# Lightning attention and a leaky-ReLU MLP on one core: the last two pairs taken together by banks and halves, and the fourth chunk's scores ahead of its key-value products

## The chip, the cores and the metric

The kernel runs on one core of a Trainium2 chip. Its time is the device time of one execution in microseconds (us). A run is one execution; a profiled execution gives the trace, whose times count from the start of its span. TensorE is PE (its weight loads PEld), VectorE DVE, ScalarE ACT, GpSimd POOL, and SP is the engine that issues most DMAs.

## The reference, cut

Two blocks follow one another. The attention has B, H, S, D = 4, 8, 768, 64 and works in blocks of 64 tokens with a decaying state:

```python
intra = einsum('bhic,bhjc->bhij', qb, kb) * Dmask          # scores, decayed
intra = einsum('bhij,bhjd->bhid', intra, vb)
inter = einsum('bhid,bhde->bhie', qb * lam_pow, kv_state)
out[:, :, sl] = intra + inter
kv_state = lam_block * kv_state + einsum('bhsd,bhse->bhde', kb * rev_pow, vb)
```

Its output, as x of 3072 tokens x 512, goes through the MLP:

```python
h = x @ w_in                      # 512 -> 2048
return maximum(0.01 * h, h) @ w_out   # 2048 -> 512
```

## The kernel before, in words

**Chunks, groups, pairs.** The attention goes by 24 chunks of 128 tokens, each with all 8 heads. Four chunks make a group of T = 512 tokens, six groups in all, and two groups make one of three rounds `pr`. The 2048 hidden units are 8 pairs `p` of 256 units.

**Number format.** Products of the MLP run in fp32r. An operand is split into a head, a low part and a middle part (`xh`, `xl`, `xm` for activations, `wh`, `wl`, `wm` for weights), and each product of the MLP is three matmuls, one per part.

**A chunk.** `load_kq` and `load_v` fetch its q, k, v on SP's queue. `transposes` turns k and q on PE and ACT copies them out (`kT`, `qT`, L429, L430); POOL scales k by its decay in place (L434). `scores(c)` then does two things in one PSUM tile `psc`: `go`, the 32 products of transposed k and q in its lower half, and `kv`, the 32 products of scaled k and v in its upper half. Which of the two is put first hangs on GOFIRST: chunks below it have `go` first. DVE takes the scores with the decay (`sc`, L467) and adds the state (L474), POOL scales the state (L477). `outputs(c)` multiplies `sc` by v and q by the state into `po`, from which ACT and DVE make the chunk's `xh`, `xl`, `xm` (L522, L523, L525). Chunks 0 to 3 are done one at a time (`alone`), later ones interleaved with the MLP's first product.

**The MLP.** `up(g, p)` is the first product (L716) with its leaky ReLU, whose result is stored to DRAM. It needs the pair's weights, which come as raw 64-bit words (`w_in`, L582) and are made into numbers by ACT (L603, L605, L607) and DVE (L609, L610, L618, L621, L636). The second product comes in two ways. `strassen` works on combinations of blocks, `plain(pr, p, gi)` on a pair as it is: `unit` loads the pair's activations for one half `gi` of the round (L815), ACT and DVE split them (L818, L821, L825) into a slot of a ring, and PE multiplies them by the pair's weights (L841): four banks c = 0 to 3, one for each 128 columns of the output, in each bank 2 x 3 matmuls of 512 columns, so 24 matmuls to a pair. The banks of `gi` = 1 are `b10`, `b2`, `b11`, `pt`.

**The end of a round.** With the last pair (p = 7) the banks are finished one by one. After each, `turn_out` has DVE transpose it from PSUM to SBUF (L909), and `store_out` writes the finished banks out by DMA (L920), four stores for each half m of 256 columns. For the very last round and half the banks go in the order 2, 3, 0, 1; banks 2 and 3 are stored together, then banks 0 and 1, and bank 1, which comes last, is done in two halves of 256 columns. These 16 stores are spread over SP, ACT and POOL by the table ENDS; all other stores go on ACT's queue.

**What sets the order of work.** Each step is put into a planner (`Plan.add`) with its engine, an estimated duration, the keys that it reads and writes, and a rank. `emit` goes through them by estimated time, each engine taking the step that can start first (rank and order of entry decide ties), and writes out the instructions in that order of estimated starts. A key names a whole tile or bank: a step waits, by the estimate, for the last writer of a key that it reads and for the readers of one that it writes. Where PE would stand still by the estimate, filler transposes (L275) are put in. The waits on the chip are set by the tiles and places that the instructions touch, in the order in which they were written out.

Of the kernel before, what the change touches and what calls it, by code (L numbers as in the profile page):

```python
# [25 lines left out]
S = 4096.0  # L26
# [10 lines left out]
class Plan:  # L37
# [23 lines left out]
    def add(self, eng, us, fn, reads=(), writes=(), rank=0.0):  # L61

        n, deps = len(self.ops), set()
        for k in reads:
            w, r = self.last.setdefault(k, [None, []])
            if w is not None:
                deps.add(w)
            r.append(n)
        for k in writes:
            w, r = self.last.setdefault(k, [None, []])  # L70
            if w is not None:
                deps.add(w)
            deps.update(r)
            self.last[k] = [n, []]
        deps.discard(n)
        ways = {eng: us} if isinstance(eng, str) else dict(zip(eng, us))
        if self.slack:
            self.more[n] = self.slack
        if self.chain is not None:
            self.chains[self.chain].append(n)  # L80
        self.ops.append((ways, fn, deps, (self.rank + rank, n), set(writes)))
# [81 lines left out]
def kernel(  # L163
# [10 lines left out]
    nc = tc.nc  # L174
    P = 128
# [6 lines left out]
    NP = d_ff // (2 * P)  # L182
    NCH = B * NCB
    GC = 4
    NG = NCH // GC
    T = GC * C
# [6 lines left out]
    TURN = 3  # L193
    SLACK, GSLACK = 4.0, 2.0
    EARLY_SLACK = 1.0
    GOFIRST = 3
    SUBL, FIRST = 0.75, -8.0

    NS = 4
    LEAD = 8.0  # L200
# [4 lines left out]
    C4 = P // 4  # L205
# [32 lines left out]
    HT = T // 2  # L238
# [42 lines left out]
    add = plan.add  # L281
# [160 lines left out]
    def scores(c):  # L442
# [16 lines left out]

        if c < GOFIRST:  # L460
            add("PE", 0.47, go, [f"kT{i}", f"qT{i}"], ["psc"])
# [322 lines left out]
    acc = {"X": flat[:2], "Z": flat[2:], "Y": [b1[0], b2], "V": [b1[1], bank["pt"]]}  # L784
    ACC = {"X": ["X0", "X1"], "Z": ["Z0", "Z1"], "Y": ["b10", "b2"], "V": ["b11", "pt"]}
# [9 lines left out]
    BANKS = [[("X", 0), ("X", 1), ("Z", 0), ("Z", 1)], [("Y", 0), ("Y", 1), ("V", 0), ("V", 1)]]  # L795
# [72 lines left out]
    def plain(pr, p, gi, lead, last=False, banks=None):  # L868

        g = 2 * pr + gi  # L870
        here = plan.rank
        plan.rank -= lead
        d = G[pr][p].rearrange("p (f h t) -> p f h t", f=2, h=2)[:, :, gi, :]
        j = unit(d, [x for x in plan.last if x[0] == "G" and x[1] in (str(2 * pr), str(2 * pr + 1)) and x[2:4] == f"{p}{gi}"], 2)
        plan.rank = here
        reads = [f"r{z}{j}" for z in "hlm"] + [f"w{z}{p}" for z in "hlm"]

        def go(fs, cs, lo=0, n=T):
            for f in fs:
                for c in cs:  # L880
                    d, i = BANKS[gi][c]
                    product(acc[d][i][:, lo:lo + n], j, f * T + lo,
                            lambda z, f=f, c=c: W[p][z][:, f * 2 * NQ + c * P:f * 2 * NQ + (c + 1) * P], first=pr == p == f == 0, n=n)

        if not last:
            add("PE", 0.227 * 24, lambda: go((0, 1), range(4)), reads, [ACC[d][i] for d, i in BANKS[gi]])
            return
        end = pr == NG // 2 - 1 and gi == 1
        for i, c in enumerate(banks):
            d, b = BANKS[gi][c]  # L890
            parts_ = 2 if end and i == 3 else 1
            for half in range(parts_):
                k = ACC[d][b] + (f"half{half}" if parts_ > 1 else "")
                n = T // parts_
                add("PE", 0.227 * 6 * (1.0 if parts_ == 1 else 0.53), lambda c=c, half=half, n=n: go((0, 1), (c,), half * n, n),
                    reads + ([ACC[d][b]] if parts_ > 1 else []), [k])
                turn_out(c, acc[d][b], [ACC[d][b], k], half * n, n)
                if i == 3 or end and i == 1:
                    cs = sorted(banks[:2] if end and i == 1 else banks[2:] if end else banks)
                    for m in ([half] if parts_ > 1 else range(2)):  # L900
                        store_out(pr, gi, m, cs, end)

    otile = gst.rearrange("p x f (b c j) -> p (x f b) c j", c=4, j=C4)

    def turn_out(c, b, keys, lo, n):
        nonlocal n_o
        n_o += 1
        o = otile[:, lo // C4:(lo + n) // C4, c, :]
        add("DVE", 0.1 + 0.6 * n / T, lambda: nc.vector.transpose(out=o, in_=b[:, lo:lo + n].rearrange("p (b i) -> p b i", i=C4)), keys,  # L909
            [f"o{c}{m}" for m in range(lo // HT, (lo + n) // HT)] + (["gs0", "gs1"] if n_o <= 4 else []), rank=-1.5)  # L910

    def store_out(pr, gi, m, cs, last):
        t0, n, w = (2 * pr + m) * T + gi * HT, HT // C4, len(cs) * C4

        ENDS = {(8, 0): "PSAP", (8, 1): "PSAP", (4, 0): "SAPP", (4, 1): "SASA"}
        QUEUES = {"S": ("DMA", 0.5, nc.sync), "A": ("ACT", 0.5, nc.scalar), "P": ("POOL", 0.65, nc.gpsimd)}

        def store(a, q):
            c0 = a * P + cs[0] * C4
            q.dma_start(out=out[t0:t0 + HT, c0:c0 + w].rearrange("(b i) j -> i b j", i=C4),  # L920
                        in_=otile[a * C4:(a + 1) * C4, m * n:(m + 1) * n, cs[0]:cs[-1] + 1, :].rearrange("i b c j -> i b (c j)"))

        for a in range(4):
            e, us, q = QUEUES[ENDS[8 if cs[0] > 1 else 4, m][a] if last else "A"]
            add(e, us, lambda a=a, q=q: store(a, q), [f"o{c}{m}" for c in cs], [], rank=-1.5 if last else 6.0)

    def copy_banks(d, s):
        for i in range(2):
# [2 lines left out]
    def add_banks(d, s):  # L931
        for i in range(2):
            y, key = w32[:, i, :], [f"w32{i}"]
            add("ACT", 0.6, lambda i=i, y=y: nc.scalar.copy(y, acc[s][i]), [ACC[s][i]], key, rank=-LEAD)
            add("DVE", 0.72, lambda i=i, y=y: nc.vector.tensor_tensor(acc[d][i], acc[d][i], y, op=ALU.add), key, [ACC[d][i]], rank=-LEAD)

    seq = [("a", 0), ("a", 1), ("a", 2), ("a", 3), ("wi", 1), ("b", 4), ("r", 4), ("up", 0, 1), ("wi", 0), ("r", 5),
# [26 lines left out]
    for pr in range(NG // 2):  # L964
# [3 lines left out]
        def n(p, gi, r=pr):  # L968
            return ("n", r, p, gi) if p < NP - 1 else ("l", r, p, gi, (0, 1, 2, 3) if gi == 0 else (2, 3, 0, 1))
# [6 lines left out]
        else:  # L976
            i = seq.index(("up", NG - 1, NP - 1))
            seq[i:i] = [n(0, 0)]
            seq += [n(0, 1), n(1, 0), n(1, 1), ("ws", 0), n(2, 0), n(2, 1), ("ws", 1), n(3, 0), n(3, 1), ("ws", 2), n(4, 0), n(5, 0), ("ws", 3), n(6, 0), n(7, 0)]
    seq += [n(p, 1) for p in range(NS, NP)]  # L980

    freed = False
    for n, x in enumerate(seq):
        plan.rank = float(n)
        steady = begin <= n and x[0] in ("r", "up", "wo")
        if x[0] in "abr":
            {"a": alone, "b": begun, "r": round_of}[x[0]](x[1])
        elif x[0] == "ls":
            load_subs(DV)
            turn(DV)  # L990
        elif x[0] == "lt":
            load_subs(sum(run(DV)))
        elif x[0] == "wi":
            w_in(x[1])
        elif x[0] == "up":
            up(*x[1:])
        elif x[0] == "wo":
            w_out(*x[1:])
        elif x[0] == "wp":
            if not freed:  # L1000
                add("DVE", 0.0, lambda: None, [], ["psc", "po", "X0", "X1", "Z0", "Z1"])
                freed = True
            w_out_parts(x[1])
        elif x[0] == "ws":
            if x[1] == 0:
                add("DVE", 0.0, free_attention, [], ATT + [f"e{z}{p}" for z in "hlm" for p in range(NS)])
            w_sums(x[1])
        elif x[0] == "fr":
            add("ACT", 0.0, free_raws, [], [f"raw{i}" for i in range(NRAW)] + ["rh4", "rl4", "rm4", "zr"])
        elif x[0] == "s":  # L1010
            strassen(*x[1:], LEAD)
        elif x[0] == "n":
            plain(*x[1:], LEAD)
        elif x[0] == "copy":
            copy_banks(*x[1:])
        elif x[0] == "add":
            add_banks(*x[1:])
        else:
            plain(*x[1:4], LEAD, True, x[4])
    plan.emit()  # L1020
# [30 lines left out]
```

## Time and profile before

| what | value |
|---|---|
| runs | 983.98, 604.32, 602.46 us; median 604.32 |
| the profiled execution | 603.61 us, its span 601.8 us |
| granted TensorE clock, mean | 0.996 |
| busy: PE, DVE, ACT, POOL | 98%, 65%, 48%, 23% of the span |
| DMA | 119.89 MB, 199 GB/s over the span |

A row of the order of time reads: start in us, duration in us (from the first start to the last end where several are merged), engine, line, operation, out<-in, form, count, and in brackets how long the engine stood idle before it and what ended that. SPq, ACTq are the queues that issue DMAs. A row of DMA issues gives out<-in, engine, count, size of each, and the median time in us from issue to landing. A row of waits gives who waited, for whom, the total in us, how often, and the longest.

### The profile page before, as it was taken

The numbers are of one execution on the slowest core, as the hardware profiler recorded it, in microseconds if no ns is written. First come the engines' busy times: TensorE is split into PE (matmuls) and PEld (weight loads), VectorE is DVE, ScalarE is ACT, GpSimd is POOL, SyncE is SP. The second block draws the span as 40 slices with busy tenths as digits, with TensorE's granted clock in tenths as the row PEclk, the third lists the DMA queues.
The fourth block names the chain that finished last, engine by engine and source line by source line (L and its number), as shares of the span: only waits on it lengthen the run. The fifth ranks groups of instructions, "written<-read, shape, count | busy, mean of one in ns | idle before, by whom it ended". The sixth has DMA issues, their size and how long they took to land.

```text
span 601.8 us, 13238 instructions
## 1 busy us (share of the span) xinstructions
PE 587.2 (98%) x5340; PEld 486.4 (81%) x5340; DVE 391.1 (65%) x533; ACT 291.7 (48%) x459; POOL 135.6 (23%) x176
## 2 busy tenths in 40 slices
PE   7899999999999999999999999999999999999995
PEld 6677888888788888888788888888888888888884
DVE  5999772534365664464279749975689595788741
ACT  4678974445555555565587754432244223252300
POOL 1654560554647374230000000000000000000002
PEclk9999999999999999999999999999999999999998
DMA  9998864795889999886688635526467456484433
GB/s 212 231 269 237 238 188 121 180 243 145 223 250 249 257 247 256 256 237 229 201 288 305 213 117 198 159 90 192 125 197 224 168 159 191 121 271 148 161 106 70
DMA packets 161357, 119.89 MB, mean 199 GB/s; under 512 B 98736, under 2 KB 137904, under 8 KB 161296
## 3 DMA queue, kind: packets, MB, share of 16 engines
q1 hardware_dynamic: 146160, 109.40, 62.3%
q10 hardware_dynamic: 12384, 5.58, 3.6%
q0 software_dynamic: 2752, 4.07, 2.7%
q8 instruction: 42, 0.69, 0.5%
q14 instruction: 19, 0.16, 0.1%
HBM read 79.17 MB, written 39.85 MB: 198 GB/s over the span
## 4 chain that ended last, share of the span: by engine, by line
PE 86%; DVE 5%; issue 4%; DMA 2%; SPq 2%; POOL 1%; ACT 1%; POOLq 0%; DVEq 0%; ACTq 0%
PE b L716 40%; PE po L841 12%; PE psc L841 11%; PE b L841 11%; PE pt L841 4%; PE po L328 4%; PE psc L328 3%; SPq L389 1%; DVE w L610 1%; DVE w L609 1%; DMA raws<-in_k_dram 1%; DMA xm<-g 1%; PE pt L418 1%; DMA att<-in_k_dram 1%; DVE att L474 1%
## 5 line engine op out<-in xcount | busy, mean ns | idle before, releaser
L716 PE MATMUL b<-xh,wh 128*128 128x512 f32 (+2 forms) x392 | 103.4, 387 | 1.1 <-ACT xh L522 0.8
L716 PE MATMUL b<-xm,wm 128*128 128x512 f32 (+2 forms) x392 | 104.0, 392 | 0.0
L716 PE MATMUL b<-xl,wl 128*128 128x512 f32 (+2 forms) x392 | 103.2, 387 | 0.6 <-DVE wl L621 0.6
L818 ACT ACTIVATE xh<-xm 128x1024 fp32r<-128x1024 f32 x45 | 47.7, 1061 | 93.4 <-DMA xm<-g 42.6
L716 PEld LDWEIGHTS b<-xh,wh 128*128 128x128 f32 x392 | 72.9, 188 | 16.3 <-ACT xh L522 0.9
L716 PEld LDWEIGHTS b<-xl,wl 128*128 128x128 f32 x392 | 72.8, 188 | 15.7 <-DVE wl L621 1.0
L716 PEld LDWEIGHTS b<-xm,wm 128*128 128x128 f32 x392 | 71.5, 188 | 14.9
L734 ACT ACTIVATE b<-b 128x512 f32<-128x512 f32 (+2 forms) x97 | 56.2, 581 | 55.6 <-PE b L716 55.5
L739 ACT ACTIVATE gs<-b 128x512 f32<-128x512 f32 (+2 forms) x97 | 57.2, 592 | 48.7 <-PE b L716 40.1
L920 POOL DMA_DIRECT2D out_dram<-gs x6 | 3.5, 588 | 319.3 <-issue 319.3
L821 DVE SCALAR_TENSOR_TENSOR xl<-xm,xh 128x1024 fp32r<-128x1024 f32 x45 | 54.8, 1218 | 30.0 <-ACT xh L818 29.2
L825 DVE SCALAR_TENSOR_TENSOR xm<-xl,xh 128x1024 fp32r<-128x1024 f32 x48 | 58.7, 1224 | 3.3
L467 DVE TENSOR_TENSOR att<-psc,att 128x512 f32<-128x512 f32 x24 | 16.5, 687 | 47.1 <-PE psc L328 47.1
L477 POOL TENSOR_TENSOR att<-att 128x256 f32<-128x256 f32 x40 | 33.7, 841 | 38.0 <-DVE att L474 37.9
L438 POOL TENSOR_TENSOR att<-att 128x512 f32<-128x512 f32 (+1 forms) x20 | 24.5, 1223 | 71.4 <-PE po L328 50.0
L389 POOL DMA_DIRECT2D att<-in_q_dram x64 | 39.7, 625 | 3.0 <-DVE att L398 1.7
L609 DVE TENSOR_SCALAR w<-w 128x512 int32<-128x512 int32 x32 | 19.3, 604 | 27.5 <-ACT w L603 27.5
L328 PEld LDWEIGHTS po<-att 64*64 64x64 f32 x1472 | 27.1, 134 | 9.5 <-issue 6.5
L610 DVE CUSTOM_DVE_ANT_0 w<-w,lows 128x1024 uint16<-128x1024 uint16 x32 | 29.8, 930 | 7.5 <-ACT lows L607 6.1
L328 PE MATMUL po<-att 64*64 64x64 f32 x1472 | 32.9, 222 | 1.2 <-DVE att L506 0.5
L841 PE MATMUL b<-xl,wl 128*128 128x512 f32 (+1 forms) x86 | 33.0, 384 | 0.0
L841 PE MATMUL b<-xm,wm 128*128 128x512 f32 (+1 forms) x86 | 33.0, 384 | 0.0
(153 smaller groups left out, 1073.8 us busy)
## 6 DMA issues: line engine op xcount, KB each, us to landing
g<-gs SPq DMA_DIRECT2D x31, 512.0 KB, 3.9
xm<-g SPq DMA_DIRECT2D x25, 512.0 KB, 4.5
xm<-b SPq DMA_DIRECT2D x23, 512.0 KB, 3.8
raws<-in_moe_w_in_dram SPq DMA_DIRECT2D x16, 512.0 KB, 5.4
raws<-in_moe_w_out_dram SPq DMA_DIRECT2D x16, 512.0 KB, 4.5
b<-gs SPq DMA_DIRECT2D x16, 512.0 KB, 4.1
att<-in_k_dram SPq DMA_DIRECT2D x48, 128.0 KB, 4.8
att<-in_v_dram SPq DMA_DIRECT2D x24, 256.0 KB, 5.0
```

The lines of the kernel that those rows point to most:

```text
L328: nc.tensor.matmul(dst[HALF[cols]], lhsT=lhsT[HALF[rows]], rhs=rhs[HALF[rows]], start=start, stop=True, skip_group_check=True)
L389: (move if nm == "k" else carry)(0.55 if nm == "k" else QSL, lambda o=o, z=z, e=nc.sync if nm == "k" else nc.gpsimd: e.dma_start(out=o.rea ...
L477: add("POOL", 0.7, lambda new=new, j=j: nc.gpsimd.tensor_tensor(state[(j + 1) % 4], new, _bc(lam_c, 2, D), op=ALU.mult), [f"st{j % 4}", "f ...
L609: add("DVE", 0.42, lambda: nc.vector.tensor_scalar(d, d, 3, None, op0=ALU.logical_shift_left), [], [key])
L610: add("DVE", 1.0, lambda: nc.vector.tensor_tensor(d, d, low, op=ALU.add), [kl], [key])
L716: nc.tensor.matmul(dst, lhsT=w[z][:, kk * 2 * P + f * P:kk * 2 * P + (f + 1) * P], rhs=x[z][:, kk, toks], start=start and kk == 0, stop=kk ...
L734: add("ACT", ns, lambda b=b: nc.scalar.activation(out=b, in_=b, func=AF.Copy, bias=0.0, scale=S + 1.0), [], [kb], rank=-1.5)
L739: add("ACT", t, lambda o=o, x=s_: nc.scalar.activation(out=o, in_=x, func=AF.Prelu, bias=0.0, scale=(1.0 + 1.0 / S) / (WS * U), alpha=0.01 ...
L818: nc.scalar.activation(out=ring[j][0], in_=g(), func=AF.Copy, bias=0.0, scale=NEAR)
L821: nc.vector.scalar_tensor_tensor(ring[j][1], g(), 1.0, ring[j][0].bitcast(F32), op0=ALU.mult, op1=ALU.subtract)
L825: nc.vector.scalar_tensor_tensor(m, l.bitcast(F32), -S, h.bitcast(F32), op0=ALU.mult, op1=ALU.add)
L841: nc.tensor.matmul(dst, lhsT=lhs(z), rhs=ring[j][z][:, col:col + n], start=first and z == 0, stop=z == 2, skip_group_check=True)
```

## The change

Three things are changed.

1. GOFIRST goes from 3 to 4: for chunk 3, too, `go` (scores) is put ahead of `kv`.
2. The last two pairs of the last half round are taken together by a new function `ending`. Both `unit`s are put in first. Then PE does banks 2 and 3 of pair 6, banks 2 and 3 of pair 7, banks 0 and 1 of pair 6, and for pair 7 the first halves (256 columns) of banks 0 and 1, then their second halves. Each finished piece is transposed; the stores follow after banks 2 and 3, after the first halves, and after the second halves. Before, pair 6 went through all four banks, then pair 7, and only the very last bank was halved.
3. The 16 stores of the end go alternately on SP's and ACT's queues ("SASA"); POOL has none. The half banks have no keys of their own any more: both halves write the bank's key.

```diff
-    GOFIRST = 3
+    GOFIRST = 4
...
+        def some(c, lo=0, n=T):
+            d, b = BANKS[gi][c]
+            add("PE", 0.227 * 6 * (1.0 if n == T else 0.53), lambda: go((0, 1), (c,), lo, n), reads, [ACC[d][b]])
+
+        if last == "parts":
+            return some
...
-        end = pr == NG // 2 - 1 and gi == 1
-        for i, c in enumerate(banks):
-            d, b = BANKS[gi][c]
-            parts_ = 2 if end and i == 3 else 1
-            for half in range(parts_):
-                k = ACC[d][b] + (f"half{half}" if parts_ > 1 else "")
...
+        for c in banks:
+            some(c)
+            turn_out(gi, c)
+        for m in range(2):
+            store_out(pr, gi, m, range(4), "AAAA")
+
+    def ending(pr, gi, first, lead):
+
+        one, two = (plain(pr, p, gi, lead, "parts") for p in (first, first + 1))
+        a, z = (2, 3), (0, 1)
+        for x in (one, two):
+            for c in a:
+                x(c)
+                if x is two:
+                    turn_out(gi, c)
+        for m in range(2):
+            store_out(pr, gi, m, a, "SASA")
+        for c in z:
+            one(c)
+        for m in range(2):
+            for c in z:
+                two(c, m * HT, HT)
+                turn_out(gi, c, m * HT, HT)
+            store_out(pr, gi, m, z, "SASA")
...
-        ENDS = {(8, 0): "PSAP", (8, 1): "PSAP", (4, 0): "SAPP", (4, 1): "SASA"}
-        QUEUES = {"S": ("DMA", 0.5, nc.sync), "A": ("ACT", 0.5, nc.scalar), "P": ("POOL", 0.65, nc.gpsimd)}
...
-    seq += [n(p, 1) for p in range(NS, NP)]
+    seq += [n(p, 1) for p in range(NS, NP - 2)] + [("end", NG // 2 - 1, 1, NP - 2)]
```

More of the change, by code (lines that the diff above doesn't have):

```diff
@@ L887, in plain @@
             return
-        end = pr == NG // 2 - 1 and gi == 1
-        for i, c in enumerate(banks):
-            d, b = BANKS[gi][c]
-            parts_ = 2 if end and i == 3 else 1
-            for half in range(parts_):
-                k = ACC[d][b] + (f"half{half}" if parts_ > 1 else "")
[L894 to L901, printed above, removed]
+        for c in banks:
+            some(c)
+            turn_out(gi, c)
@@ L903, with turn_out @@
     otile = gst.rearrange("p x f (b c j) -> p (x f b) c j", c=4, j=C4)
-    def turn_out(c, b, keys, lo, n):
+    def turn_out(gi, c, lo=0, n=T):
         nonlocal n_o
         n_o += 1
-        o = otile[:, lo // C4:(lo + n) // C4, c, :]
-        add("DVE", 0.1 + 0.6 * n / T, lambda: nc.vector.transpose(out=o, in_=b[:, lo:lo + n].rearrange("p (b i) -> p b i", i=C4)), keys,
+        d, i = BANKS[gi][c]
+        b, o = acc[d][i], otile[:, lo // C4:(lo + n) // C4, c, :]
+        add("DVE", 0.1 + 0.6 * n / T, lambda: nc.vector.transpose(out=o, in_=b[:, lo:lo + n].rearrange("p (b i) -> p b i", i=C4)), [ACC[d][i]],
@@ L910, in turn_out, with store_out @@
             [f"o{c}{m}" for m in range(lo // HT, (lo + n) // HT)] + (["gs0", "gs1"] if n_o <= 4 else []), rank=-1.5)
-    def store_out(pr, gi, m, cs, last):
+    def store_out(pr, gi, m, cs, queues):
         t0, n, w = (2 * pr + m) * T + gi * HT, HT // C4, len(cs) * C4
-        ENDS = {(8, 0): "PSAP", (8, 1): "PSAP", (4, 0): "SAPP", (4, 1): "SASA"}
-        QUEUES = {"S": ("DMA", 0.5, nc.sync), "A": ("ACT", 0.5, nc.scalar), "P": ("POOL", 0.65, nc.gpsimd)}
         def store(a, q):
@@ L921, in store @@
                         in_=otile[a * C4:(a + 1) * C4, m * n:(m + 1) * n, cs[0]:cs[-1] + 1, :].rearrange("i b c j -> i b (c j)"))
-        for a in range(4):
-            e, us, q = QUEUES[ENDS[8 if cs[0] > 1 else 4, m][a] if last else "A"]
-            add(e, us, lambda a=a, q=q: store(a, q), [f"o{c}{m}" for c in cs], [], rank=-1.5 if last else 6.0)
+        for a, x in enumerate(queues):
+            e, q = {"S": ("DMA", nc.sync), "A": ("ACT", nc.scalar)}[x]
+            add(e, 0.5, lambda a=a, q=q: store(a, q), [f"o{c}{m}" for c in cs], [], rank=6.0 if len(cs) == 4 else -1.5)
     def copy_banks(d, s):
@@ L1017 @@
             add_banks(*x[1:])
+        elif x[0] == "end":
+            ending(*x[1:], LEAD)
         else:
```

## The prediction

> **What bounds the kernel now.** I read the page's busy table first, then busy time by stretch, then the order of time in the two stretches that the change touches, then the waits and the landings of the DMAs there.
>
> ```profile
> span 601.8 us, 13238 instructions
> PE 587.2 (98%) x5340; PEld 486.4 (81%) x5340; DVE 391.1 (65%) x533; ACT 291.7 (48%) x459; POOL 135.6 (23%) x176
> 0.00:47.50 47.50, 40.37 (x810) 32.26 (x810) 37.92 (x67) 29.79 (x54) 21.65 (x26) 1.00 0.94 234
> 47.50:330.00 282.50, 281.38 (x3355) 234.34 (x3356) 160.64 (x272) 169.66 (x296) 110.48 (x144) 1.00 0.81 229
> 330.00:590.00 260.00, 260.00 (x1149) 215.29 (x1148) 189.59 (x191) 92.24 (x110) 0.00 (x0) 1.00 0.53 166
> 595.45:601.80 6.35, 0.00 (x0) 0.00 (x0) 0.78 (x2) 0.00 (x0) 2.04 (x4) 0.67 0.59 134
> ```
>
> The stretch rows give length, then busy time of PE, PE's weight loads, DVE, ACT and POOL, granted clock, DMA share and GB/s. PE is the bound: from 47.5 to 590 us it idles 1.1 us in all. It is without work in only two places, the first 47.5 us (47.50 - 40.37 = 7.1 us) and the tail after its last matmul (6.35 us). The change adds or removes next to no matmul work, so it can win only there, and 13.5 us, some 2% of the time, is more than everything that could be won. About 2% is also what a measurement of this kernel can tell from no change.
>
> **The start: chunk 3's scores ahead of its key-value products.** These rows are the fourth chunk (number 3) in order of time, and the landing time (last number, us after issue) of its v load.
>
> ```profile
> 18.66 0.46 SPq L403 DMA_DIRECT2D att<-in_v_dram  x1
> att<-in_v_dram SPq DMA_DIRECT2D x1, 256.0 KB, 5.3
> 20.30 0.59 ACT L429 COPY att<-b 128x512 f32<-128x512 f32 x1
> 21.75 1.06 POOL L434 TENSOR_TENSOR att<-att 128x512 f32<-128x512 f32 x1
> 21.83 0.42 DVE L474 TENSOR_TENSOR att<-att,psc 128x256 f32<-128x256 f32 x1
> 22.03 0.66 PE L418 MATMUL pt<-att 128*128 128x128 f32 x4
> 24.06 1.16 PE L328 MATMUL psc<-att 64*64 64x64 f32 x64 [1.37 <-DVE xl L523]
> 25.28 0.69 DVE L467 TENSOR_TENSOR att<-psc,att 128x512 f32<-128x512 f32 x1 [1.32 <-PE psc L328]
> 8.40 0.69 PE L328 MATMUL psc<-att 64*64 64x64 f32 x32
> ```
>
> PE stands still for 1.37 us before 24.06 and then does both halves, 64 products, in 1.16 us. The row names DVE's xl, but chunk 3's products read nothing of it. What they read is k scaled (POOL, over at 22.81), the bank psc (DVE's last reader over at 22.25) and v, which was issued at 18.66 and lands 5.3 us later, at 23.96. So v is what PE waits for. The scores don't need v: their transposed k is there at 20.89 (the transposed q before it) and psc at 22.25, and PE is free from 22.69. Put first, they fit into the wait, and after v's landing only the other half is left. A half alone takes 0.69 us (the row at 8.40), so psc is finished at about 24.06 + 0.69 = 24.75 instead of 25.22. Gain 0.47 us, and no more, since L467 reads a tile that both halves write: it has to wait for the key-value half, whichever goes first.
>
> Whether 0.47 us reaches the end depends on what follows. The rows show who is the bound behind it.
>
> ```profile
> 26.81 1.64 DVE L621 SCALAR_TENSOR_TENSOR wl<-wh,w 128x1024 fp32r<-128x1024 f32 x1
> 28.71 2.10 PE L716 MATMUL b<-xh,wh 128*128 128x512 f32 x8 [0.78 <-ACT xh L522]
> 30.62 0.67 ACT L603 ACTIVATE w<-raws 128x512 f32<-128x512 f32 x1 [1.40 <-DMA raws<-in_moe_w_in_dram]
> 31.34 0.66 PE L418 MATMUL po<-att 128*128 128x128 f32 x4 [0.53 <-DVE xl L523]
> 36.68 0.79 ACT L605 ACTIVATE lows<-raws 128x512 uint16<-128x512 uint32 x1 [1.71 <-DMA raws<-in_moe_w_in_dram]
> DVE att L474 <- POOL att L477: 0.5, 1, 0.5
> 47.52 1.20 PE L716 MATMUL b<-xl,wl 128*128 128x512 f32 x4 [0.61 <-DVE wl L621]
> ```
>
> From 25.28 to 47.5 DVE idles only 0.5 us (on POOL) and PE's waits end on DVE or on ACT behind it, so DVE's chain sets the start of the steady stretch at 47.52, and DVE's 1.32 us of idle time before L467 is where it can be shortened. Against it: ACT waits twice for a raw weight load, 1.40 and 1.71 us, and what ends on a landing doesn't move with DVE. Bounds: 0 where those landings decide, 0.56 where the half costs half of 1.16. I take 0.4, as DVE's row has no wait on ACT's converted weights.
>
> **The tail: the last two pairs by banks and halves.** Now the end, in order of time.
>
> ```profile
> 576.98 1.23 DVE L825 SCALAR_TENSOR_TENSOR xm<-xl,xh 128x1024 fp32r<-128x1024 f32 x1
> 584.30 0.39 PE L841 MATMUL b<-xh,wh 128*128 128x512 f32 x1
> 589.74 0.39 PE L841 MATMUL b<-xh,wh 128*128 128x512 f32 x1
> 592.46 0.39 PE L841 MATMUL b<-xh,wh 128*128 128x512 f32 x1
> 593.82 0.28 PE L841 MATMUL b<-xh,wh 128*128 128x256 f32 x1
> 595.13 0.28 PE L841 MATMUL b<-xm,wm 128*128 128x256 f32 x1
> 591.30 0.72 DVE L909 STREAM_TRANSPOSE gs<-b 128x512 f32<-128x512 f32 x1 [13.09 <-PE b L841]
> 595.45 0.78 DVE L909 STREAM_TRANSPOSE gs<-b 128x256 f32<-128x256 f32 x2 [0.71 <-PE b L841]
> 596.34 1.17 SPq L920 DMA_DIRECT2D out_dram<-gs  x2
> L920 ACTq DMA_DIRECT2D out_dram<-gs x5: 372/413/703, 593.4 to 596.9; - x5
> L920 POOL DMA_DIRECT2D out_dram<-gs x6: 582/584/607, 594.0 to 596.9; - x6
> out_dram<-gs ACTq DMA_DIRECT2D x1, 64.0 KB, 3.8
> DMA to landing us min/median/max: 2.0/2.6/3.8
> out_dram<-gs ACTq DMA_DIRECT2D x8, 128.0 KB, 2.4
> ```
>
> Pair 6 starts at 584.30, pair 7 at 589.74, the last bank's two halves at 593.82; PE ends at 595.13 + 0.28 = 595.41. Both half transpositions start only at 595.45, behind the last matmul, although the first half's products started 0.72 us before the second's: they lie in one bank and DVE waited 0.71 us for PE. So eight stores of the last two banks are issued in a heap, SP's between 596.34 and 597.51, ACT's last at 596.9, and that last one takes 3.8 us to land, at 600.7. The span ends 1.1 us later.
>
> What PE pays. Pair 7 is now wanted after 12 of pair 6's matmuls, at 587.02, not at 589.74; its last part is ready at 576.98 + 1.23 = 578.2, so nothing waits. Full matmuls come every (592.46 - 589.74) / 12 = 0.227 us, halves every (595.13 - 593.82) / 11 = 0.119 us. Bank 0 in halves costs 12 x 0.119 - 6 x 0.227 = +0.07 us. Taken by halves first, bank 0's second half must wait until DVE has read its first half: that read takes 0.39 us (half of 0.78) and lies behind bank 1's first half, 6 x 0.119 = 0.71 us. Cost 0, cover to spare about 0.3 us; without that cover it would be some 0.4 us twice. PE ends at 595.48.
>
> What DVE and the queues save. Only one half transposition is left behind PE: 595.48 + 0.04 + 0.39 = 595.91, 0.32 us before today's 596.23. The half before it is read while PE works, so the four stores of the first half are issued from about 594.6 (its last matmul starts 11 x 0.119 after 592.46 and takes 0.28, then 0.04, 0.39 and 0.11). The last four come two to a queue: with 0.11 us from transposition to issue and 0.41 us for the first (ACT's median), the last is issued at 596.43, against 596.9 now. Banks 2 and 3 are finished at 589.74 instead of 592.46 and their stores are long through. POOL's issue of 0.58 us each leaves the tail altogether.
>
> How long the last store then takes to land isn't in the trace. Bounds: 3.8 us, if crowding isn't the cause (landing 600.2, gain 0.5), and 2.0 us, the least of the sixteen (598.4, gain 2.3). I take 2.6, their median, a little above the 2.4 us that stores of double the size took on a single queue at 576 to 579 us: landing 599.0, gain 1.7. The Trainium skill's page "DMA: Bandwidth & Descriptors" (section "Anatomy of one DMA — SWDGE (gpsimd) path") gives a DMA a fixed 2.0 us and 1 us for each 436 KB, so an estimate by it is 2.15 us for 64 KB and a forecast 0.45 us lower than mine; its fit is for DMAs issued by POOL, and the landing of 3.8 us differs from it.
>
> **The sum.** The profiled execution took 603.61 us (span 601.8, 1.8 around it). 603.61 - 0.4 (start) - 1.7 (tail, PE's +0.07 included) = **601.5 us**. The three runs shown were 602.46, 604.32 and 983.98, median 604.32: the profiled one lies between the first two, which differ by 1.9 us, so I allow 0.9 us each way for the run.
>
> **Rivals.**
> (a) The start gives nothing: the raw loads that ACT waits for (1.40, 1.71 us) decide, and scores merely sit earlier in an idle slot. For: DMA share 0.94 up to 47.5 us. Against: DVE without a wait for ACT. 603.61 - 1.7 = 601.9.
> (b) The tail gives little: the last stores take 3.8 us whatever lies before them, gain 0.5, start 0.4: 602.7. For: no row shows a last store without a crowd. Against: half of the sixteen landed within 2.6.
> (c) Slower: the order on every engine is written out by the planner, which re-times all after chunk 3's products. If that puts a raw weight load on SP's queue behind a pair of q loads, it is issued up to 2.28 us later (row below), ACT, which waits for it with nothing in hand, is as late, and so are DVE's chain and PE at 47.52; all of it is lost, for PE is full afterwards. It decides from 1.7 us on, the tail's gain. One pair: 603.61 + 2.28 - 1.7 = 604.2; two pairs (2.28 + 1.66): 605.9. Against: the estimate of the fourth chunk moves by at most one half, and a swap of two neighbours with nothing else late leaves the order as it was.
>
> ```profile
> 21.09 2.28 SPq L353 DMA_DIRECT2D att<-in_q_dram  x2
> 25.99 1.66 SPq L353 DMA_DIRECT2D att<-in_k_dram  x2
> ```
>
> (d) The halves stall PE: second halves wait for DVE, 0.4 us twice, tail gain 0.9: 602.3. The Trainium skill's "PSUM — Partial Sum Buffer" (section "PSUM bank collisions raise a hardware error") wants PSUM guarded by bank and not by address, which the 0.71 us wait at 595.45 agrees with; it makes these waits real, but by the rows they are covered.
>
> **Chances.** Forecast 0.45, (a) 0.2, (b) 0.13, (c) 0.14, (d) 0.08. Range: low end 603.61 - 0.56 - 2.3 less 0.9 for the run is 599.9, of which I keep 600.0; high end by (c) with one pair and part of the run's spread, 604.7. Faster by over 2% would need 12 us, nearly all of PE's idle time: 0.02. Slower by over 2% would need several loads displaced at once: 0.02. Within 2%: 0.96.
>
> **What would show it.** Start: a psc row of 32 products before v's landing, L467's wait down from 1.32 to about 0.85 us, PE's steady work from about 47.1. If L467 starts earlier but the steady stretch doesn't, it is (a). Tail: 24 matmuls of 256 columns at 0.12 us without a gap, one transposition of 0.39 us behind the last, last issue near 596.0 (596.43 less the start's gain), landing 2.6 us later, span 599.7. Gaps between the half matmuls mean (d); a last landing near 3.8 us means (b). A changed order of SP's loads with ACT's waits on raw weights above 2 us means (c), and then the forecast is wrong in sign.

## The result, and the profile after

The changed kernel takes 601.21 us (median of 15 runs, 600.31 to 602.62) against 603.08 us before, measured beside it. The ratio is 0.9968 with a 95% interval of 0.9959 to 0.9977, so 1.9 us (1.4 to 2.5) are won; the one run of 983.98 us, of the kernel before, is left out of the ratio. The forecast was 601.5, 2.1 us under the profiled execution of before.

The page's head and busy time by stretch of the changed kernel (columns as before):

```profile
span 599.1 us, 13248 instructions
PE 588.3 (98%) x5346; PEld 487.3 (81%) x5346; DVE 393.8 (66%) x534; ACT 290.6 (49%) x459; POOL 132.3 (22%) x170
0.00:47.50 47.50, 41.41 (x809) 32.73 (x810) 37.82 (x67) 29.23 (x53) 21.30 (x26) 1.00 0.96 232
47.50:330.00 282.50, 282.22 (x3361) 235.10 (x3361) 164.37 (x273) 169.59 (x297) 110.95 (x144) 1.00 0.81 230
```

The span is 2.7 us shorter, more than the runs as a whole gained; PE idles 0.28 us from 47.5 to 330 us where it idled 1.12 us before. In the executions profiled below this idle time lies anywhere between 0.28 and 1.46 us, and in the three of the changed kernel itself it is 0.28, 0.68 and 1.02, so that part is the execution's and not the change's. To keep it out, the tail is counted from one mark that all kernels share, the start of pair 5's last matmul, to the end of the span. Now the order of time at the end:

```profile
583.16 0.39 PE L841 MATMUL pt<-raws,wm 128*128 128x512 f32 x1
583.39 0.39 PE L841 MATMUL b<-xh,wh 128*128 128x512 f32 x1
587.67 0.72 DVE L926 STREAM_TRANSPOSE gs<-b 128x512 f32<-128x512 f32 x1 [10.36 <-PE b L841]
591.55 0.28 PE L841 MATMUL b<-xh,wh 128*128 128x256 f32 x1
592.46 0.45 DVE L926 STREAM_TRANSPOSE gs<-b 128x256 f32<-128x256 f32 x1 [2.72 <-PE b L841]
592.98 0.37 PE L841 MATMUL b<-xh,wh 128*128 128x256 f32 x1
593.19 0.28 PE L841 MATMUL b<-xl,wl 128*128 128x256 f32 x1
594.38 0.28 PE L841 MATMUL b<-xm,wm 128*128 128x256 f32 x1
594.70 0.45 DVE L926 STREAM_TRANSPOSE gs<-b 128x256 f32<-128x256 f32 x1 [0.27 <-PE b L841]
L934 ACTq DMA_DIRECT2D out_dram<-gs x1: 469/469/469, 595.6 to 595.6; - x1
DMA to landing us min/median/max: 1.8/2.1/2.2
```

The last two rows are the last issue on ACT's queue, and landing times of the last eight stores. Banks 2 and 3 are transposed from 587.67 instead of 591.30, one transposition instead of two lies behind PE's last matmul (that ends at 594.66, the transposition at 595.15), and the last stores land within 2.2 us, where one took 3.8 before. From the mark to the end of the span it is 599.1 - 583.16 = 15.9 us, against 601.8 - 584.08 = 17.7 before (pair 5's last matmul starts 0.22 us ahead of pair 6's first, at 584.30). So the tail gave 1.8 us. By the rounded rows 0.4 of it come from the earlier last issue (12.8 us after the mark before, 12.4 now), 1.6 from its shorter landing (3.8 before, 2.2 now), and 0.2 are lost again, as the span ends 1.3 instead of 1.1 us after that landing. The 1.8 us are the gain of the runs within their interval, and leave nothing for the start that could be told.

### The profile page after: what moved, and what is told of

It reads as the page before. It is cut to its first block, busy times and chain, and to the rows that moved or that the text cites. A ratio compares the mean times of both kernels' runs of the same rounds, so it can differ in the third digit from the quotient of the medians.

```text
span 599.1 us, 13248 instructions
## 1 busy us (share of the span) xinstructions
PE 588.3 (98%) x5346; PEld 487.3 (81%) x5346; DVE 393.8 (66%) x534; ACT 290.6 (49%) x459; POOL 132.3 (22%) x170
## 4 chain that ended last, share of the span: by engine, by line
PE 95%; DMA 2%; DVE 1%; ACT 0%; issue 0%; SPq 0%
PE b L716 44%; PE b L841 14%; PE po L841 13%; PE psc L841 11%; PE pt L841 5%; PE po L328 4%; PE psc L328 3%; DMA att<-in_k_dram 2%; PE pt L418 1%; DMA att<-in_q_dram 1%; PE po L418 0%; PE b L275 0%; DVE w L609 0%; ACT att L430 0%; DVE att L438 0%; DVE att L467 0%
## 5 line engine op out<-in xcount | busy, mean ns | idle before, releaser
L716 PE MATMUL b<-xh,wh 128*128 128x512 f32 (+2 forms) x392 | 103.5, 387 | 0.9 <-ACT xh L522 0.8
L716 PE MATMUL b<-xm,wm 128*128 128x512 f32 (+2 forms) x392 | 104.0, 392 | 0.0
L716 PE MATMUL b<-xl,wl 128*128 128x512 f32 (+2 forms) x392 | 103.2, 387 | 0.0
L716 PEld LDWEIGHTS b<-xh,wh 128*128 128x128 f32 x392 | 72.8, 188 | 16.3 <-ACT xh L522 0.9
L716 PEld LDWEIGHTS b<-xl,wl 128*128 128x128 f32 x392 | 72.9, 188 | 14.8
L716 PEld LDWEIGHTS b<-xm,wm 128*128 128x128 f32 x392 | 71.5, 188 | 14.9
L467 DVE TENSOR_TENSOR att<-psc,att 128x512 f32<-128x512 f32 x24 | 16.5, 689 | 47.4 <-PE psc L328 47.3
L438 POOL TENSOR_TENSOR att<-att 128x512 f32<-128x512 f32 (+1 forms) x20 | 25.3, 1265 | 72.3 <-PE po L328 50.4
L610 DVE CUSTOM_DVE_ANT_0 w<-w,lows 128x1024 uint16<-128x1024 uint16 x32 | 31.6, 986 | 7.3 <-ACT lows L607 5.9
L841 PE MATMUL b<-xh,wh 128*128 128x512 f32 (+1 forms) x88 | 33.5, 380 | 0.0
```

What stands on the lines that cost most here:

```text
L438: add(eng, us, lambda: e.tensor_tensor(o, x, _bc(pow_q, 2, 2)[:, :, m, :], op=ALU.mult), ["fq", dep], [f"qsT{i}"])
L610: add("DVE", 1.0, lambda: nc.vector.tensor_tensor(d, d, low, op=ALU.add), [kl], [key])
L716: nc.tensor.matmul(dst, lhsT=w[z][:, kk * 2 * P + f * P:kk * 2 * P + (f + 1) * P], rhs=x[z][:, kk, toks], start=start and kk == 0, stop=kk ...
L841: nc.tensor.matmul(dst, lhsT=lhs(z), rhs=ring[j][z][:, col:col + n], start=first and z == 0, stop=z == 2, skip_group_check=True)
```

## The experiments

Eleven experiments follow the first measurement, every ratio against the kernel before on the same chip; e8_changed and e11_changed repeat the changed kernel, e9_end repeats e2_end. e1 to e3 share one chip, e4, e5, e8 and e9 a second, e6, e7, e10 and e11 a third. The last column is the tail, from pair 5's last matmul to the end of the span, in one profiled execution each.

| kernel | what | median us | before | ratio (95% interval) | tail, us |
|---|---|---|---|---|---|
| before | | | | | 17.7 |
| changed | first measurement | 601.21 | 603.08 | 0.9968 (0.9959 to 0.9977) | 15.9 |
| e1_scores | scores alone | 603.95 | 603.82 | 1.0008 (0.9994 to 1.0023) | 17.8 |
| e2_end | ending alone | 600.84 | 603.82 | 0.9952 (0.9940 to 0.9963) | 16.0 |
| e3_late_kv | changed, key-value products late | 602.32 | 603.82 | 0.9975 (0.9966 to 0.9984) | 15.9 |
| e8_changed | changed again | 601.40 | 603.24 | 0.9962 (0.9947 to 0.9977) | 16.0 |
| e9_end | ending alone again | 600.88 | 603.24 | 0.9959 (0.9941 to 0.9978) | 15.9 |
| e4_no_halves | changed, no halves | 601.84 | 603.24 | 0.9978 (0.9959 to 0.9997) | 17.4 |
| e5_one_bank | changed, halves bank by bank | 602.35 | 603.24 | 0.9979 (0.9966 to 0.9992) | 17.4 |
| e6_pool | changed, POOL in the stores | 601.73 | 603.66 | 0.9967 (0.9956 to 0.9979) | 15.9 |
| e7_pairs | changed, pair after pair | 603.13 | 603.66 | 0.9989 (0.9979 to 0.9999) | 17.2 |
| e10_scores_q4 | changed, scores ahead of q's transposes too | 601.47 | 603.66 | 0.9969 (0.9957 to 0.9981) | 15.9 |
| e11_changed | changed again | 601.76 | 603.66 | 0.9967 (0.9954 to 0.9980) | 16.0 |

### Which of the two parts: e1_scores, e2_end, e8_changed, e9_end

e1_scores is the kernel before with one line changed, e2_end and e9_end are the changed kernel with it changed back:

```diff
-    GOFIRST = 3      # e1_scores, on the kernel before
+    GOFIRST = 4
-    GOFIRST = 4      # e2_end and e9_end, on the changed kernel
+    GOFIRST = 3
```

> The kernel before with GOFIRST = 4 alone; the tail is as before. Theory of the forecast: chunk 3's psc is finished half a pass (0.47 us) earlier against v's landing, DVE's wait ahead of L467 falls from 1.32 to about 0.85 us, and 0.4 us of it reaches the end: 0.4 us faster than before. Rival (a): L467 is as much earlier, but raw weight loads decide the steady start: 0.0 us. The profile of the changed kernel, in which pair 6 began 0.91 us earlier than before, if that is all the start: 0.9 us faster.

> The changed kernel with GOFIRST = 3, so the new ending alone. Forecast: 1.7 us faster than before, and from pair 6's first matmul to the end of the span about 15.7 us (15.71 in the changed kernel, 17.53 before). Rival (a) expects the whole change, 1.9 us. If the start carries 0.9 us of the change's 1.9, this run is only 1.0 us faster.

> The changed kernel as it is, on one chip with the ending alone (e9_end). It was 1.9 us faster than before on its first chip, the ending alone 2.9 us on another. If the scores' place is worth nothing (rival (a)), both are the same here, within 0.5 us. If the forecast's 0.4 us are there, this one is 0.4 us the faster of the two. If the earlier pair of results is to be taken at its word, it is 1 us the slower.

> The ending alone again (GOFIRST = 3), beside e8_changed on one chip. Forecast: 1.7 us faster than before; by e2_end 2.9 us.

Measured: the scores alone show no gain (0.5 us slower, from 0.4 faster to 1.4 slower), the ending alone brings 2.9 us on one chip and 2.5 on another, where the whole change brings 2.3: no difference that could be told. By the middle values of the ratios the scores' place costs rather than gains; the intervals don't decide that. The tail explains 1.8 of each. That e2_end's interval (2.2 to 3.6 us) doesn't reach down to that was not settled; the same kernel's second interval (1.3 to 3.6) does.

Why the scores bring nothing is in the order of time around chunk 3, first of e1_scores, then of e8_changed:

```profile
22.00 0.44 PE L418 MATMUL pt<-att 128*128 128x128 f32 x2
23.82 0.44 PE L418 MATMUL pt<-att 128*128 128x128 f32 x2 [1.37 <-DMA att<-in_q_dram]
24.18 1.90 PE L328 MATMUL psc<-att 64*64 64x64 f32 x64
26.14 0.69 DVE L467 TENSOR_TENSOR att<-psc,att 128x512 f32<-128x512 f32 x1 [2.21 <-PE psc L328]
```

```profile
18.98 1.16 PE L328 MATMUL psc<-att 64*64 64x64 f32 x64 [0.73 <-DVE att L474]
23.15 0.66 PE L418 MATMUL pt<-att 128*128 128x128 f32 x4
23.74 1.16 PE L328 MATMUL psc<-att 64*64 64x64 f32 x64
24.99 0.68 DVE L467 TENSOR_TENSOR att<-psc,att 128x512 f32<-128x512 f32 x1
```

In e1_scores the transposes of chunk 4's q, which stand ahead of the scores in PE's order, wait 1.37 us for that q to land, so the scores can't start before 24.18 and all 64 products run in one go again. They take 1.90 us instead of 1.16, at a granted clock of 0.58 (last section), which makes L467 later still. In e8_changed chunk 2 is later (its products start at 18.98, at 17.86 in the profile of before), PE reaches chunk 3's place at 23.74, and v has landed by then: again one go, no wait. Where v lands clearly last, the scores go into the gap, as in the first profile of the changed kernel (its first two rows are v's issue and the time to its landing):

```profile
19.40 0.46 SPq L403 DMA_DIRECT2D att<-in_v_dram  x1
att<-in_v_dram SPq DMA_DIRECT2D x1, 256.0 KB, 5.2
23.45 0.69 PE L328 MATMUL psc<-att 64*64 64x64 f32 x32
24.70 0.69 PE L328 MATMUL psc<-att 64*64 64x64 f32 x32 [0.55 <-POOL att L477]
25.45 0.69 DVE L467 TENSOR_TENSOR att<-psc,att 128x512 f32<-128x512 f32 x1 [0.66 <-PE psc L328]
47.79 1.07 PE L716 MATMUL b<-xl,wl 128*128 128x512 f32 x4
```

There DVE's wait did fall from 1.32 to 0.66 us, but v came 0.6 us later than in the profile of before (19.40 + 5.2 against 18.66 + 5.3), and L467 started at 25.45 instead of 25.28. Counted from v's landing (issue plus landing time), the half pass is won: L467 starts 0.9 us behind it in seven profiles with the scores first (changed, e4, e5, e6, e7, e10, e11), and 1.3 to 1.4 us behind it in the three with the key-value products first (before, e2, e9). e1_scores and e8_changed, above, are the exceptions. But v itself lands at 24.0 to 24.7 us in those seven and at 23.6 to 24.0 in those three, which takes the half pass away again. It is issued at 18.7 to 19.4 us, some 3 us ahead of chunk 3's products, so nothing in the rows lays its later landing to the swap. Over all profiled executions L467 starts at 25.2 us on average with key-value products first (25.28, 24.99, 25.39) and at 25.3 with scores first (25.45, 26.14, 24.99, 25.13, 24.95, 25.21, 25.56, 25.05; 25.2 without e1_scores' 26.14).

### Does a shift there reach the end: e3_late_kv

```diff
         def kv():
+            if c == 3:
+                busy(20)
```

> The changed kernel with 20 filler transposes (about 2.1 us at 0.107 each) ahead of chunk 3's key-value products, so psc of chunk 3 is finished some 2.1 us later, less what of PE's wait for v it covers (0.55 us): about 1.6 us. It asks what a delay at this place costs at the end. Forecast's theory (DVE's chain from L467 to the steady start decides): 1.3 to 1.6 us slower than the changed kernel, so about 0.3 us faster than before. Rival (a), raw loads decide: under 0.5 us slower than the changed kernel, about 1.5 us faster than before.

```profile
25.58 0.69 PE L328 MATMUL psc<-att 64*64 64x64 f32 x32
26.34 0.69 DVE L469 TENSOR_TENSOR att<-psc,att 128x512 f32<-128x512 f32 x1 [2.41 <-PE psc L328]
48.42 1.07 PE L718 MATMUL b<-xl,wl 128*128 128x512 f32 x4
```

L467 (here L469) starts at 26.34, 1.0 us later than the average of the others, not 1.6, and the steady stretch's matmuls with the low part start at 48.42 instead of 47.0 to 47.9. So lateness passes nearly whole in this execution and in e1_scores (26.14 and 48.16). The runs are by ratio 0.4 to 0.8 us slower than the changed kernel (0.9975 against its 0.9968, 0.9962 and 0.9967), with intervals that overlap: between the two theories for a shift of 1.0 us, and no clear verdict for either. The changed kernel did not run on e3's chip. Against the ending alone, which did (e2_end, 0.9952), it is 1.4 us slower, beyond both intervals; so lateness here does cost something, and how much is open. Among the executions with L467 from 24.95 to 25.56 the low-part matmuls start anywhere from 46.96 to 47.88 without a trend. What else sets that, raw weights' landings or others, was not separated.

### Scores ahead of the transposes of q too: e10_scores_q4

The transposes of chunk 4's q are put out right behind chunk 3's scores instead of ahead of them; nothing else moves.

```diff
+            turn_q = lambda: go(tq, [pt[:, y, :] for y in range(HP)])
-            add("PE", 0.44, lambda: go(tq, [pt[:, y, :] for y in range(HP)]), [f"q{i}"], ["pt"])
+            add("PE", 0.44, (lambda: held.append(turn_q)) if c == GC else turn_q, [f"q{i}"], ["pt"])
...                                                  # at the end of scores' go()
+            if held:
+                held.pop()()
```

> The changed kernel with one swap in PE's order: chunk 3's scores also ahead of the transposes of chunk 4's q, which stood ahead of them and waited 1.37 us for that q's landing in e1_scores. If that wait is why the scores' place gave nothing: scores done by about 23 us in every execution, L467 at most 0.7 us after v's landing, and 0.2 to 0.4 us faster than the changed kernel. If what follows (landings of raw weights) decides anyway: no difference.

> The changed kernel again, as the measure for the other three on this chip: 1.9 to 2.3 us faster than before, 15.9 us from the last matmul of pair 5 to the end.

```profile
22.23 0.69 PE L328 MATMUL psc<-att 64*64 64x64 f32 x32 [0.19 <-DVE att L479]
24.24 0.69 PE L328 MATMUL psc<-att 64*64 64x64 f32 x32 [0.73 <-DMA att<-in_v_dram]
24.99 0.69 DVE L472 TENSOR_TENSOR att<-psc,att 128x512 f32<-128x512 f32 x1 [1.11 <-PE psc L328]
```

The swap does what it was made for: the scores are through before 23 us and L467 (here L472) starts 0.1 us after the key-value half. The time is that of the changed kernel on the same chip (0.9969 against 0.9967). So even a sure place for the scores is worth nothing that these runs show; with intervals of 0.7 us either way they couldn't have told the expected 0.2 to 0.4. The second half stays where v's landing puts it.

### The tail taken apart: e4_no_halves, e5_one_bank

e4_no_halves turns banks 0 and 1 of pair 7 into one piece each; e5_one_bank keeps the halves and takes both of bank 0 first (a further key that `two` gets there keeps bank 1 behind them in the planner):

```diff
         for m in range(2):                    # as changed
             for c in z:
                 two(c, m * HT, HT)
                 turn_out(gi, c, m * HT, HT)
             store_out(pr, gi, m, z, "SASA")
...                                            # e4_no_halves
+        for c in z:
+            two(c)
+            turn_out(gi, c)
...                                            # e5_one_bank
+        for c in z:
+            for m in range(2):
+                two(c, m * HT, HT, [ACC[d][b]] if c != z[0] else [])
+                turn_out(gi, c, m * HT, HT)
...                                            # both
+        for m in range(2):
+            store_out(pr, gi, m, z, "SASA")
```

> The changed kernel with pair 7's banks 0 and 1 each in one piece of 512 columns. PE is 0.2 us shorter, but a transposition of 0.72 instead of 0.45 us lies behind the last matmul and all eight stores of 64 KB follow in a heap, four to a queue: 0.52 MB at the tail's 190 GB/s take 2.8 us. From pair 6's first matmul to the end 17.0 us against 15.7, so 1.3 us slower than the changed kernel. If halves are worth nothing (only the order of banks and the queues count): within 0.3 us of it.

> The changed kernel with the halves in another order: both halves of bank 0, then both of bank 1. If PE and DVE are kept apart by whole banks, each second half waits until DVE has read the first: 0.28 + 0.04 + 0.45 us in place of 0.12, so two gaps of some 0.65 us in PE and the end 1.3 us later than in the changed kernel. If halves of one bank don't wait for one another: no gap, within 0.3 us of it.

The end of e4_no_halves, mark first:

```profile
582.58 0.39 PE L841 MATMUL pt<-raws,wm 128*128 128x512 f32 x1
593.46 0.39 PE L841 MATMUL b<-xm,wm 128*128 128x512 f32 x1
593.88 0.72 DVE L926 STREAM_TRANSPOSE gs<-b 128x512 f32<-128x512 f32 x1 [0.64 <-PE b L841]
L934 SPq DMA_DIRECT2D out_dram<-gs x4: 316/458/465, 594.6 to 596.0; - x4
DMA to landing us min/median/max: 1.9/2.5/2.6
```

PE is through 0.2 us sooner after the mark, but the transposition takes 0.72 us, four stores to a queue are issued until 596.0 + 0.46, and the last lands 2.6 us after issue. Tail 600.0 - 582.58 = 17.4 us, 1.5 more than the changed kernel's 15.9; expected were 1.3.

PE and DVE in e5_one_bank:

```profile
592.98 0.28 PE L841 MATMUL b<-xm,wm 128*128 128x256 f32 x1
593.81 0.39 PE L841 MATMUL b<-xh,wh 128*128 128x256 f32 x1 [0.54 <-DVE gs L928]
596.05 0.39 PE L841 MATMUL b<-xh,wh 128*128 128x256 f32 x1 [0.54 <-DVE gs L928]
597.06 0.45 DVE L928 STREAM_TRANSPOSE gs<-b 128x256 f32<-128x256 f32 x1 [1.07 <-PE b L841]
```

Both second halves wait for DVE's reading of the first half of their own bank: from the start of one matmul to that of the next it is 0.83 us instead of 0.12. With the matmul behind each gap also 0.1 us late, two such gaps put PE's last matmul 12.74 us after the mark (596.74 - 584.00) instead of 11.22: 1.5 us, and the tail is 1.5 longer too. So by turns between banks the waits of whole banks are hidden; bank by bank they are paid in full.

The runs agree in direction only: by ratio both kernels are 1.0 us slower than the changed one on their chip (0.9978 and 0.9979 against 0.9962), with intervals that overlap, and 1.3 us faster than before where the tails say 0.3. The sizes of 1.5 us stand on the tails of one profiled execution each.

### The queues and the order of the pairs: e6_pool, e7_pairs

```diff
-            store_out(pr, gi, m, z, "SASA")                    # e6_pool; banks 2 and 3 "PSAP"
+            store_out(pr, gi, m, z, ("SAPP", "SASA")[m])
...
             for c in a:                                        # e7_pairs
                 x(c)
                 if x is two:
                     turn_out(gi, c)
+            if x is one:
+                for c in z:
+                    one(c)
-        for c in z:
-            one(c)
```

> The changed kernel with the queues of before (PSAP and PSAP for banks 2 and 3, SAPP for the first halves, SASA for the second). POOL starts 0.6 us after SP and ACT and takes 0.58 us for each, so its two stores of the first halves are issued until about 2.0 us after the transposition and land some 2.8 to 3.3 us later, about when the last store lands now. From the last matmul of pair 5 to the end 15.9 to 16.3 us against 15.9 in the changed kernel: 0 to 0.4 us slower. If leaving POOL is what made the tail short: 1 us slower or more.

> The changed kernel with pair 6 taken whole ahead of pair 7, as before, and pair 7 then by banks 2 and 3, first halves, second halves. Banks 2 and 3 are finished 2.7 us later, so their eight stores (0.52 MB, 2.8 us at 190 GB/s) run into those of the first halves (0.26 MB). If the DMAs' rate sets the end: the last landing 0.5 to 0.9 us later than in the changed kernel. If only the last four stores count: within 0.2 us of it.

POOL's stores and all landings of the last banks in e6_pool:

```profile
L934 POOL DMA_DIRECT2D out_dram<-gs x4: 582/582/584, 591.5 to 594.5; - x4
DMA to landing us min/median/max: 1.8/2.1/2.3
```

With POOL back in its places the time and the tail are the changed kernel's. In the new order POOL's 0.58 us an issue cost nothing, and its stores land as soon as the others. The store that took 3.8 us before was one of ACT's, in the heap. What leaving POOL would have done in the order of before, no run shows.

In e7_pairs (order of time with the landing of SP's first store and the semaphore waits of its queue, then stretches with PE, weight loads, DVE, ACT, POOL, clock, DMA share and GB/s):

```profile
593.48 4.39 SPq L935 DMA_DIRECT2D out_dram<-gs  x8
out_dram<-gs SPq DMA_DIRECT2D x1, 64.0 KB, 2.1
L935 SPq EVENT_SEMAPHORE  x2: 17/17/17, 595.5 to 597.0; - x2
595.68 0.45 DVE L927 STREAM_TRANSPOSE gs<-b 128x256 f32<-128x256 f32 x1 [0.27 <-PE b L841]
595.00:596.00 1.00, 0.64 (x6) 0.44 (x4) 0.73 (x2) 0.00 (x0) 0.00 (x0) 1.00 1.01 197
596.00:597.00 1.00, 0.00 (x0) 0.00 (x0) 0.13 (x1) 0.00 (x0) 0.00 (x0) 1.00 1.00 198
597.00:598.00 1.00, 0.00 (x0) 0.00 (x0) 0.00 (x0) 0.00 (x0) 0.00 (x0) 1.00 1.01 212
598.00:599.00 1.00, 0.00 (x0) 0.00 (x0) 0.00 (x0) 0.00 (x0) 0.00 (x0) 1.00 0.98 199
```

Everything is computed as in the changed kernel, PE and DVE end as long after the mark, and yet the tail is 1.2 us longer than the changed kernel's 16.0 in e11 (expected 0.5 to 0.9; by the runs 1.3 us slower, with intervals that just overlap). All 16 stores, 1.05 MB, follow in one train: SP's queue issues from 593.48 to 597.87, though the last pieces are ready at 596.13, and the DMAs are full (share 1.0 at about 200 GB/s) from 595 to 599. The last issues are late because each queue waits for its own earlier stores: SP's fifth store is held by a semaphore until about 595.5, when its first one lands (593.48 + 2.1), its seventh until 597.0, when its third lands (594.36 + 2.6). So in this trace no queue has more than four stores on their way. Whether full DMAs or this limit sets the end was not separated; either way it is the stores still ahead of the last ones that cost. The order by banks takes half of these bytes out of the end.

By the tails, the order by banks without halves (e4_no_halves) gives 0.3 us against before, halves without the order by banks (e7_pairs) 0.5, both together 1.8. The parts need each other: without the halves eight stores instead of four wait for the last transposition, without the order by banks eight more stand ahead of the last ones.

## Why the prediction was right, point by point

- **Bound.** Right: the change could win only where PE has no work, and the gain lies in the tail. That only about 2% could be told from no change was too coarse: the intervals here are 0.1 to 0.2% either way, and 0.3% is told.
- **Start, 0.4 us.** Wrong in size: no gain (e1_scores 0.5 us slower, from 0.4 faster to 1.4 slower). The step "So v is what PE waits for" holds in ten of twelve executions (all but e1_scores and e8_changed; e3_late_kv, with its delay, not counted), and there the half pass is worth about what was forecast: L467 starts 0.9 us after v's landing instead of 1.3 to 1.4. The step that failed is the next one, that 0.4 us of it reach the end. v's landing moves by more than the half pass from execution to execution, so L467 starts as late as before on average, and no run shows an earlier end. One profile showed one of these landings. Rival (a) was right that the start gives nothing; whether for its reason, that landings of raw weights decide, stays open, since a later L467 does show in the steady start (e1_scores, e3_late_kv).
- **PE's price, +0.07 us.** From pair 6's first matmul to PE's end 11.11 us before (584.30 to 595.41), 11.27 after (583.39 to 594.66): +0.16, of which 0.09 is the wait in the next point.
- **Cover for the bank's wait, 0.3 us.** Wrong: there is none to spare. PE's next matmul starts at 592.98, the one after it 0.21 us later instead of 0.12, and DVE had read until 592.91. The working took 0.71 us for bank 1's half, but bank 0's last matmul ends 0.16 us into it, DVE starts 0.04 us later and takes 0.45, not 0.39 (that was half of a row of two that overlap). What is left is 0.06 us, and 0.09 was paid once. Mechanism (d) is real, as e5_one_bank shows, and nearly all of it is hidden.
- **Issue and landing.** The last issue was forecast 12.13 us after pair 6's first matmul; the last is issued at 595.6, 12.2 us after 583.39. Landing 2.2 us, forecast 2.6. The Trainium skill's page "DMA: Bandwidth & Descriptors" (section "Anatomy of one DMA — SWDGE (gpsimd) path") has a fit, for DMAs issued by POOL, by which 64 KB take an estimated 2.15 us. The trace agrees, with 1.8 to 2.2 us for the last eight stores, which come from SP and ACT four at a time; in a crowd it differs (up to 2.6 with the eight of e4_no_halves, 2.8 with the sixteen on two queues of e7_pairs, 3.8 with the sixteen on three queues of before).
- **Leaving POOL.** Named as part of the gain, without a price of its own; in the new order worth nothing (e6_pool).
- **The sum.** Tail 1.7 forecast, 1.8 measured; start 0.4 forecast, none measured; 2.1 against 1.9 (1.4 to 2.5). That the time came so near, 601.5 against 601.21, is partly luck: the start's 0.4 us didn't come, but the sum began at the profiled execution's 603.61, 0.5 us above the median of before, and the one made up for the other. Within the tail the landing gave 0.4 us more than forecast, and PE's price and the later end behind the landing took 0.3 of that back.
- **(c).** Didn't happen: up to the ending, every engine's instructions stand in the order of before, but for the swap itself.

## What to carry to other kernels

Look at the last microseconds of a kernel as a train of stores: what counted in this kernel was how many bytes were still to be moved when the last product was done. So finish whole output regions early and leave only small pieces for the end, halved by turns over two banks so that the reading of one hides under the products of the other. A gap that one profile shows behind a load isn't a gain yet: look at several executions for what comes last, and for how far that landing moves by itself.

## What the runs showed of the hardware that was not expected

- The granted clock fell at this place in one execution, and the length of the wait before it doesn't explain it. In e1_scores PE waited 1.37 us at 22.4 to 23.8 us; the granted clock was then 0.58 from 24 to 26 us and 0.78 on average from 26 to 30, and chunk 3's 64 products took 1.90 us. Where they ran in one go in the other profiles they took 1.16 to 1.39. In the profile of before a wait of the same 1.37 us ended at 24.06 and the clock stayed at 1.00. What lowered it in e1_scores stays open. First e1_scores, then before:

```profile
24.00:26.00 2.00, 2.00 (x66) 1.73 (x65) 0.00 (x0) 1.60 (x3) 1.05 (x1) 0.58 0.91 215
24.00:26.00 2.00, 1.86 (x69) 1.58 (x69) 0.72 (x2) 1.09 (x3) 1.07 (x1) 1.00 0.67 148
```

- Executions with the same order of instructions there differ by up to 1.2 us in PE's idle time between 47.5 and 330 us (0.28 in the changed kernel, 1.46 in e5_one_bank), in single waits of 0.3 to 0.8 us, some of which (L716 at 64.7 us of before, 0.31 us) no semaphore in the profile explains.
